# Turning the last four row tiles of x and dO by transposing DMA through DRAM instead of by TensorE, in a gated spectral and GEGLU backward kernel

## The chip, the cores and the metric

One core of a Trainium2 chip runs one launch. The metric is device time in microseconds, the median of several runs; the kernel before took 1384.09 us (three runs, 1383.98 to 1384.36). The profile is one execution of 1384.02 us, whose recorded span is 1382.2 us. The core's engines work at the same time and wait for each other by semaphores: PE (TensorE, matrix products; "PEld" is its weight load), DVE (VectorE), ACT (ScalarE), POOL (GpSimd), and SP (SyncE), which here does nothing but issue DMA transfers. "Granted clock" is the share of full speed that TensorE was given; it was 1.00 throughout.

## The reference

The kernel returns the output of a gated sum of two branches and the gradients of it with respect to x and all weights:

```python
x = A_x                                                   # [2048, 576], bf16
g = sigmoid((x * gate_w).sum(-1, keepdims=True))
a = irfft2(rfft2(x) * (w_r + 1j * w_i))                   # spectral branch
b = (gelu(x @ w_gate) * (x @ w_up)) @ w_down              # GEGLU branch, 4608 inner columns
out = g * a + (1 - g) * b
# returned: out, and the vjp for grad_out (called dO below) with respect to
# x, w_r, w_i, w_gate, w_up, w_down and gate_w
```

For the GEGLU branch each inner column needs the row of x and of dO multiplied with weights. TensorE contracts over the partition, so it needs x and dO with their 576 columns on the partitions: xT and dOT, the "turned" forms. The 2048 rows are cut into 16 row tiles of 128 rows (row p*16+t is row p of tile t), the 576 columns into four interleaved chunks of 128 (column 4*m+r is row m of chunk r) and a tail of 64.

## The kernel before

The inner columns are worked through in 18 groups of 256 (`NG`); each group takes the 16 row tiles in four slots of four tiles (`NPR = 4`, loop variable `m`). A slot multiplies (`H_mm`), evacuates on ACT (`H_da`, `H_act`), and works out the GELU derivative on DVE in two halves (`H_ew1`, `H_ew2`), with a sigmoid on ACT between them. The weight gradients of a group (`W_units`) are filled in between the products of the next group. Group 0 has no such filler: there x and dO are still being turned, four row tiles per slot.

```python
    def H_ew1(g, tiles, da):
        xb, q, hu = tiles
        s = ewt("s", g)
        V.tensor_scalar(s[:], q[:], A_GELU, 1.0, op0=ALU.mult, op1=ALU.add)
        V.tensor_tensor(s[:], xb[:], s[:], op=ALU.mult)
        V.tensor_scalar(q[:], q[:], 6.0 * A_GELU * C_GELU, 2.0 * C_GELU, op0=ALU.mult, op1=ALU.add)
        dH = keep.tile([P, 4, 2, FG], BF16, tag="dH", name="dH")
        V.tensor_tensor(dH[:, :, 0, :], da[:], hu[:], op=ALU.mult)
        return s, dH
    ...
    def H_ew2(g, m, tiles, s, dH, da):
        xb, q, hu = tiles
        one = g < 2 or m == 2
        if one:
            om = xb if g < 2 else ewt("sg", g)
            nc.scalar.activation(s[:], s[:], ACT.Sigmoid, scale=2.0 * C_GELU)
        ...
        def products():
            V.tensor_tensor(dHu, da[:], xb[:], op=ALU.mult)
            V.tensor_tensor(A[:], xb[:], hu[:], op=ALU.mult)
        V.tensor_tensor(xb[:], xb[:], s[:], op=ALU.mult)
        if g < 2:
            products()
        V.tensor_tensor(q[:], xb[:], q[:], op=ALU.mult)
        if one:
            V.tensor_scalar(om[:], s[:], -1.0, 1.0, op0=ALU.mult, op1=ALU.add)
        V.tensor_tensor(om[:], om[:], q[:], op=ALU.mult)
        if g >= 2:
            products()
        V.tensor_tensor(om[:], om[:], s[:], op=ALU.add)
        V.tensor_tensor(dHg, dHg, om[:], op=ALU.mult)
        # then, as a later step: A, dHu and dHg are stored to DRAM
```

Turning by TensorE: three items per four tiles, chunks 0 and 1, chunks 2 and 3, and the tail. Each item needs one of two PSUM buffers "pf" and a copy out of it, on DVE or ACT.

```python
    def titems(src, dst, t0, ps, copies, n=4):
        def item(k, cs):
            def f():
                tp_ = ps[k](BF16).rearrange("p (j t m) -> p j t m", j=2, t=4)
                for j, c in enumerate(cs):
                    for tt in range(n):
                        if c < 4:
                            nc.tensor.transpose(tp_[:, j, tt, :], src[:, t0 + tt, eo(c)], ident[:])
                        ...                          # the tail: one transpose per tile
                copies[k](dst[:, cs[0]:cs[0] + len(cs), t0:t0 + n, :], tp_[:, 0:len(cs), 0:n, :])
            return f
        return [item(k, cs) for k, cs in enumerate(((0, 1), (2, 3), (4,)))]
```

`gate(k)` makes the gate's logits of tiles 4k to 4k+3 out of xT, into another "pf" buffer. A slot of group 0 (engines take instructions in the order in which they are recorded here):

```python
                do2 = items(dB, dOT, m + 2, AC, AC, VC)               # dO, two slots ahead
                x1 = items(xn, xT, m + 1, AC if m else VC, VC, VC)    # x, one slot ahead
                z, xy_full = H_mm(g, m, [lambda: gate(0)] if m == 0 else rest, ...)
                da = H_da(g, m, z)
                ...
                elif m < NPR - 1:
                    early, mid_, late_ = x1[:1], x1[1:], []
                for f in early:
                    f()
                xy = xy_full(0)
                for f in mid_:
                    f()
                if held and m < NPR - 1:
                    held.pop()()                     # H_ew2 of the slot before
                for part in (1, 0):
                    H_act(0, xy, tiles, part)
                if held:
                    held.pop()()
                xy = xy_full(1, between)
                for part in range(2):
                    H_act(1, xy, tiles, part)
                ...
                if m < NPR - 1:
                    gate(m + 1)
                ...
                if m + 2 < NPR:
                    do2[0]()
                    rest = do2[1:]
                state += [*H_ew1(g, tiles, da), da]
                held.append(sigs)
            ...
            if m < 3 and g + 1 < NG:                 # weights of the next group
                for part in ((0, 1), (2,), (3,))[m]:
                    load_w(g + 1, part)
```

`load_w` already turns w_down in the way that the change takes for x and dO: part 1 is a transposing DMA into an SBUF tile, part 2 writes that tile to a DRAM scratch, part 3 reads it back so that four interleaved chunks come out (a row of the scratch is a column of the weight; "(p r) f -> p r f", r=4). All of these are issued from SP. The tile framework hands out eight DMA semaphores in turn, so a DMA of SP is not issued before the one eight before it has landed.

The masked tables ("tails", a helper `D4[2]`): two memsets and 16 small multiplications on POOL, used from the seventh slot on; recorded in the first slot.

Of the kernel before, what the change touches and what calls it, by code (L numbers as in the profile page):

```python
# [11 lines left out]
BF16 = mybir.dt.bfloat16  # L12
# [22 lines left out]
FCH = FG // P  # L35
NUNIT = 18
IMM = bass.MemoryType

# [237 lines left out]
def kernel(  # L276
# [22 lines left out]
    o5v = out_5[0:512, :].rearrange("(c p) f -> p c f", p=P)  # L299
    scr = [[dram.tile([4, P, FF], BF16, name=f"scr{k}_{m}") for m in range(T // 4)] for k in range(3)]  # L300
    wscr = [dram.tile([512, FG], BF16, name=f"wscr{k}") for k in range(2)]
    a_scr = dram.tile([S, D], BF16, name="a_scr")
# [44 lines left out]
    def load_do(t0, n=4):  # L347
        LD.dma_start(dB[:, t0:t0 + n, :], do_v[:, t0:t0 + n, :])

    ident = res.tile([P, P], BF16, name="ident")  # L350
    make_identity(nc, ident[:])
# [8 lines left out]
    for k in range(1, 4):  # L360
        load_do(4 * k)
        load_x(4 * k)
    tb = iotas(nc, res, unit)

# [137 lines left out]
    def H_ew2(g, m, tiles, s, dH, da):  # L502
        xb, q, hu = tiles
        one = g < 2 or m == 2
        if one:
            om = xb if g < 2 else ewt("sg", g)
            nc.scalar.activation(s[:], s[:], ACT.Sigmoid, scale=2.0 * C_GELU)
        else:
            om, s = s, ewt("sg", g)
            nc.scalar.activation(s[:], om[:], ACT.Sigmoid, scale=2.0 * C_GELU)  # L510
            nc.scalar.activation(om[:], om[:], ACT.Sigmoid, scale=-2.0 * C_GELU)
# [6 lines left out]
        V.tensor_tensor(xb[:], xb[:], s[:], op=ALU.mult)  # L518
        if g < 2:
            products()  # L520
# [3 lines left out]
        V.tensor_tensor(om[:], om[:], q[:], op=ALU.mult)  # L524
        if g >= 2:
            products()
# [164 lines left out]
    def turned(h):  # L691

        def f():
# [9 lines left out]
            if h == 1:  # L703
                V.tensor_copy(tb.BT[:].rearrange("p v m -> p (v m)"), tp_[:, 1, 0:2 * P])
            tb.RT.extend(o[:, k, :] for k in range(8))
        return f

# [262 lines left out]
    def opening():  # L970
        x0 = titems(xn, xT, 0, (pgtile, pgtile, phtile), (VC, VC, VC))
        for f in (x0[2], x0[0], x0[1]):
            f()
        parity()
        D4[2]()

# [69 lines left out]
    for g in range(NG):  # L1046
# [3 lines left out]
        for m in range(NPR):  # L1050
# [15 lines left out]
            if g == 0:  # L1066
# [8 lines left out]
                if m == 0:  # L1075
                    early, mid_, late_ = do1[:2], [do1[2], x1[0]], x1[1:]
                elif m < NPR - 1:
                    early, mid_, late_ = x1[:1], x1[1:], []
                else:
                    early, mid_, late_ = [], [], []  # L1080
# [20 lines left out]
                if m == 0:  # L1101
                    build_R(nc, tb, unit, 4)
                    columns_B(nc, tb, res)
                elif m == 1:
                    next(makeB)
                if m < NPR - 1:
                    gate(m + 1)
# [3 lines left out]
                if m + 2 < NPR:  # L1111
                    do2[0]()
                    rest = do2[1:]
                state += [*H_ew1(g, tiles, da), da]
                held.append(sigs)
            else:
# [31 lines left out]
                at, k, free = 0.0, k0, 0.0  # L1148
                last = getattr(upcoming(n - k0)[-1], "last", 0.0) if n > k0 else 0.0
                tables = {6: 2}.get(pr)  # L1150
                for i, (w, f) in enumerate(jobs):
                    if k < n and (at >= max(min(total * k / n - 0.45, total - last - 0.9 * (n - 1 - k)), free) or len(jobs) - i <= n - k):
                        free = at + (1.7 if wide() else 0.0)
# [19 lines left out]
            if m < 3 and g + 1 < NG:  # L1173
                for part in ((0, 1), (2,), (3,))[m]:
                    load_w(g + 1, part)
            if done[0] == n_slots or (pr >= wgT_from and pr % 2 == 0 and len(wgT_all) < 20):
                load_wgT()
# [245 lines left out]
```

## Time and profile before

| what | value |
|---|---|
| time, median of three runs | 1384.09 us (1383.98 to 1384.36) |
| profiled span | 1382.2 us |
| busy: PE, PEld, DVE, ACT, POOL | 99%, 66%, 57%, 51%, 19% of the span |
| 0 to 60 us: PE, DVE, ACT, POOL busy | 56.47, 49.28, 47.57, 26.31 us |
| 60 to 120 us: PE, DVE, ACT, POOL busy | 57.25, 49.86, 48.29, 7.29 us |
| 950 to 1382.2 us: PE, DVE, ACT busy | 428.62, 89.39, 13.92 us |

Lines are named by their number in the kernel (L399 is a transposing matmul of chunks 0 to 3, L405 one of the tail; L406 their copy out of PSUM; L423 the gate; L444 and L449 the product z with dOT; L453 and L460 the product xy with xT; L472, L479, L481, L482 the evacuations on ACT; L487 to L528 the chain on DVE; L507 the sigmoid). Matmuls are pipelined and their ends are modelled: a matmul of 512 columns shows 379 ns but 16 of them in a row start within 3.45 us. Gaps are therefore read from the starts.

In a line of the timeline stand the start in us, the duration in us, engine, line, operation, what is written and read, the shape, and how many instructions were merged; in brackets the idle time before it and what ended it. In the chain of waits (the chain of work that ended last, in order of time) stand start, duration, engine, what is written, line, and the number of instructions.

### The profile page before, as it was taken

To read this page: it belongs to the slowest core of one execution; us is meant where nothing else is said; L and a number is where in the kernel's file an instruction comes from. 1 tells how busy PE (TensorE), PEld (TensorE's weight loads), DVE (VectorE), ACT (ScalarE), POOL (GpSimd) and SP (SyncE) were. 2 spreads that over 40 slices of the span, in tenths; PEclk is the share of its full clock that TensorE was granted. 3 is DMA by queue.
4 is the path that set the end of the run, shared out by engine and by line. 5 is a ranking of instruction groups with operands and counts; after the bars stand their busy time and mean duration, and the time that the engine had idled before them with its cause. 6 is when DMAs were issued, how large, how long until landed. Compare 5 with 4: busy or idle time off the path is not lost.

```text
span 1382.2 us, 25988 instructions
## 1 busy us (share of the span) xinstructions
PE 1363.2 (99%) x10186; PEld 908.5 (66%) x10272; DVE 783.2 (57%) x1514; ACT 701.6 (51%) x1300; POOL 259.8 (19%) x513
## 2 busy tenths in 40 slices
PE   9999999999999999999999999999999999999998
PEld 6556656566556556556656566556777777777776
DVE  7887777865988877885676766550001642122101
ACT  7877777768877877866766767651000000000000
POOL 7001110132445444331110111110000110000000
PEclk9999999999999999999999999999999999999999
DMA  7434444466466665555556556659999997787773
GB/s 234 126 88 136 128 131 119 120 169 158 129 162 159 161 160 150 143 156 151 135 157 154 159 158 166 168 128 274 196 190 197 235 193 164 158 161 168 155 150 88
DMA packets 512423, 218.95 MB, mean 158 GB/s; under 512 B 312010, under 2 KB 503180, under 8 KB 512300
## 3 DMA queue, kind: packets, MB, share of 16 engines
q1 hardware_dynamic: 495178, 191.89, 59.3%
q0 software_dynamic: 14912, 24.24, 6.1%
q8 instruction: 80, 1.31, 0.4%
q10 hardware_dynamic: 2210, 1.15, 0.4%
q14 instruction: 43, 0.35, 0.1%
HBM read 45.51 MB, written 98.30 MB: 104 GB/s over the span
## 4 chain that ended last, share of the span: by engine, by line
PE 92%; ACT 3%; DVE 2%; DMA 1%; issue 1%; ACTq 0%; SPq 0%; DVEq 0%
PE acc L1273 31%; PE wps L590 16%; PE xy L460 16%; PE wps L572 10%; PE z L444 8%; PE wps L604 2%; PE xy L453 2%; PE z L449 2%; DMA wgu<-in_B_w_up_dram 1%; DMA xn<-in_A_x_dram 1%; PE pf L914 1%; PE pf L840 1%; PE pf L751 1%; PE pf L633 1%; PE pf L916 1%
## 5 line engine op out<-in xcount | busy, mean ns | idle before, releaser
L1273 PEld LDWEIGHTS <-pin 128*128 128x128 bf16 x3456 | 337.5, 98 | 86.3 <-issue 0.3
L590 PE MATMUL wps<-dH,xn 128*128 128x512 bf16 x1135 | 270.0, 379 | 0.9
L460 PE MATMUL xy<-wgu,xT 128*128 128x512 bf16 x1083 | 258.6, 380 | 8.2 <-issue 6.8
L460 PEld LDWEIGHTS <-xT 128*128 128x128 bf16 x1152 | 106.4, 98 | 132.9 <-issue 24.8
L590 PEld LDWEIGHTS <-xn 128*128 128x128 bf16 x1152 | 111.4, 98 | 118.4 <-issue 0.6
L1290 ACT COPY bo<-acc 128x288 f32<-128x288 f32 x32 | 12.8, 399 | 305.0 <-PE acc L1273 271.6
L572 PE MATMUL wps<-dB,A 128*128 128x288 bf16 x1152 | 153.3, 286 | 0.1
L597 POOL DMA_DIRECT2D out_dram<-dw x134 | 72.8, 547 | 421.9 <-ACT dw L541 380.4
L1273 PE MATMUL acc<-wgT,pin 128*128 128x288 bf16 x1152 | 143.8, 286 | 0.0
L1273 PE MATMUL acc<-wuT,pin 128*128 128x288 bf16 x1152 | 143.6, 286 | 0.0
L1273 PE MATMUL acc<-wd_all,pin 128*128 128x288 bf16 x1152 | 142.6, 286 | 0.0
L444 PE MATMUL z<-wdT,dOT 128*128 128x256 bf16 x1152 | 137.7, 273 | 0.0
L572 PEld LDWEIGHTS <-A 128*128 128x128 bf16 x1152 | 112.0, 98 | 33.0 <-issue 0.3
L472 ACT ACTIVATE da<-z,omg 128x256 bf16<-128x256 f32 x288 | 112.0, 471 | 31.9 <-PE z L449 31.8
L444 PEld LDWEIGHTS <-dOT 128*128 128x128 bf16 x1152 | 112.3, 98 | 21.6 <-issue 0.6
L1345 DVE SCALAR_TENSOR_TENSOR f32t<-gwf,dlog,b16t 128x576 f32<-128x576 f32 x16 | 13.1, 818 | 171.8 <-DMA b16t<-dxa_scr 171.8
L481 ACT CAST xb<-xy 128x512 bf16<-128x512 f32 x144 | 85.0, 590 | 48.2 <-PE xy L460 48.2
L479 ACT ACTIVATE q<-xy 128x512 bf16<-128x512 f32 x144 | 87.8, 613 | 17.0 <-PE xy L460 13.5
L482 ACT CAST hu<-xy 128x512 bf16<-128x512 f32 x144 | 87.4, 607 | 0.0
L518 DVE TENSOR_TENSOR xb<-xb,sg 128x1024 bf16<-128x1024 bf16 x48 | 33.1, 690 | 85.8 <-ACT sg L510 85.7
L541 ACT CAST dw<-wps 128x512 bf16<-128x512 f32 x72 | 42.3, 590 | 54.8 <-PE wps L590 52.4
L1304 DVE SCALAR_TENSOR_TENSOR b16t<-b16t,g,f32t 128x576 bf16<-128x576 bf16 x16 | 13.1, 818 | 98.1 <-DMA b16t<-a_scr 97.9
(239 smaller groups left out, 1700.3 us busy)
## 6 DMA issues: line engine op xcount, KB each, us to landing
scr<-dH SPq DMA_DIRECT2D x144, 256.0 KB, 3.4
scr<-A SPq DMA_DIRECT2D x72, 256.0 KB, 2.5
out_dram<-dw POOLq DMA_DIRECT2D x134, 64.0 KB, 2.5
wd_all<-in_B_w_down_dram SPq DMA_DIRECT2D x3, 1728.0 KB
out_dram<-dwd POOLq DMA_DIRECT2D x34, 144.0 KB, 2.9
scr_p<-Vt SPq DMA_DIRECT2D x32, 145.0 KB, 2.8
wgu<-in_B_w_gate_dram SPq DMA_DIRECT2D x18, 256.0 KB, 4.1
wgu<-in_B_w_up_dram SPq DMA_DIRECT2D x18, 256.0 KB, 3.4
```

Source lines behind the costliest of these rows:

```text
L444: nc.tensor.matmul(zo(t), lhsT=dOT[:, ci, t, :], rhs=wdT[:, ci, :], start=(t % 4 < 2 and ci == 0), stop=False)
L460: nc.tensor.matmul(xy[k][:, t % 2, :], lhsT=xT[:, ci, t, :], rhs=wgu[:, ci, :], start=False, stop=(ci == 3))
L472: nc.scalar.activation(da[:, t, :], z[:, t % 2, t // 2, :], ACT.Copy, scale=omg32[:, 4 * m + t:4 * m + t + 1])
L479: nc.scalar.activation(q[:, h, :], xy[:, :, 0:FG], ACT.Square)
L481: nc.scalar.copy(xb[:, h, :], xy[:, :, 0:FG])
L482: nc.scalar.copy(hu[:, h, :], xy[:, :, FG:2 * FG])
L518: V.tensor_tensor(xb[:], xb[:], s[:], op=ALU.mult)
L541: wcopy[0](out, in_)
L572: nc.tensor.matmul(wps[:, :288], lhsT=tl(0, t)[:, fch * P:(fch + 1) * P], rhs=dB[:, t, h * 288:(h + 1) * 288], start=(t == 0), stop=(t == ...
L590: nc.tensor.matmul(wps[:].rearrange("p a b -> p (a b)"), lhsT=xn[:, t, c * P:(c + 1) * P], rhs=kt[t // 4][1][:, t % 4].rearrange("p k f -> ...
L597: wst[0].dma_start(ov[:, c, fsl], dw[:, k, :])
L1273: nc.tensor.matmul(acc[:, :288], lhsT=src[:, r, :], rhs=w_of(r)[:, h * 288:(h + 1) * 288], start=(first and r == 0), stop=(last and r == F ...
```

## The change

Of the last four row tiles (12 to 15) the chunks 0 to 3 of x and of dO are no longer turned by TensorE. Eight transposing DMAs, one per tile and tensor, are issued right behind the loads; each brings 128 rows by 512 columns, turned, into one of four SBUF tiles. In slot 0 the four tiles are written to DRAM, in slot 1 they are read back into xT and dOT, four interleaved chunks at a time. The tails of these tiles are still turned by TensorE. This is for TensorE, ACT and DVE to have less to do in group 0. Besides, the masked tables are recorded in slot 1 and no longer in slot 0; the second group's chain on DVE takes the order that the third and later groups have (products later, into a tile of its own); and the rule that spreads the transform's units over a slot's weight gradient work is given one more hint.

```diff
+LT = T - 4
...
+    turn = [[dram.tile([512, 2 * P], BF16, name=f"turn{k}_{u}") for u in range(2)] for k in range(2)]
...
+    byq = {}
+    def load_turned(part):
+        for k, (v, dst) in enumerate(((do_v, dOT), (x_v, xT))):
+            for u in range(2):
+                if part == 0:
+                    tmp = byq[k, u] = unit([4, 2, P], name="turn")
+                    for j in range(2):
+                        LD.dma_start_transpose(tmp[:, :, j, :], v[:, LT + 2 * u + j, 0:512])
+                elif part == 1:
+                    LD.dma_start(turn[k][u][:].rearrange("(c p) f -> p c f", p=P),
+                                 byq[k, u][:].rearrange("p c t m -> p c (t m)"))
+                else:
+                    LD.dma_start(dst[:, 0:4, LT + 2 * u:LT + 2 * u + 2, :].rearrange("p r t m -> p r (t m)"),
+                                 turn[k][u][:].rearrange("(p r) f -> p r f", r=4))
...
     for k in range(1, 4):
         load_do(4 * k)
         load_x(4 * k)
+    load_turned(0)
     tb = iotas(nc, res, unit)
...
-            om = xb if g < 2 else ewt("sg", g)
+            om = xb if g == 0 else ewt("sg", g)
...
-        if g < 2:
+        if g == 0:
             products()
...
-        if g >= 2:
+        if g > 0:
             products()
...
+        f.room, f.last = 1.7, 2.0                    # the unit that turns the transform's tables
...
         parity()
-        D4[2]()
...
                 elif m < NPR - 1:
-                    early, mid_, late_ = x1[:1], x1[1:], []
+                    early, mid_, late_ = (x1[:1], x1[1:], []) if m < NPR - 2 else ([], x1[2:], [])
...
                 elif m == 1:
                     next(makeB)
+                    D4[2]()
...
                 if m + 2 < NPR:
-                    do2[0]()
-                    rest = do2[1:]
+                    rest = do2[1:] if m + 3 < NPR else do2[2:]
+                    if len(rest) > 1:
+                        do2[0]()
...
-                last = getattr(upcoming(n - k0)[-1], "last", 0.0) if n > k0 else 0.0
+                ups = upcoming(n - k0)
+                last = getattr(ups[-1], "last", 0.0) if ups and (n < 5 or hasattr(ups[-1], "wide")) else 0.0
+                due = [total - last - sum(getattr(u, "room", 0.9) for u in ups[j:-1]) for j in range(len(ups))]
...
-                    if k < n and (at >= max(min(total * k / n - 0.45, total - last - 0.9 * (n - 1 - k)), free) or len(jobs) - i <= n - k):
+                    if k < n and (at >= max(min(total * k / n - 0.45, due[k - k0]), free) or len(jobs) - i <= n - k):
...
                 for part in ((0, 1), (2,), (3,))[m]:
                     load_w(g + 1, part)
+                if g == 0 and m < 2:
+                    load_turned(m + 1)
```

## The prediction

> **What bounds the kernel now.** I read the page's busy times first, then the chain of waits, the timelines and the list of waits of the first 120 us, because everything that the change touches lies there: the instruction streams of the two programs, laid side by side without line numbers, differ only in slots 0 to 7 and in the place of four weight gradient products near the unit that turns the transform's tables.
>
> ```profile
> PE 1363.2 (99%) x10186; PEld 908.5 (66%) x10272; DVE 783.2 (57%) x1514; ACT 701.6 (51%) x1300; POOL 259.8 (19%) x513
> ```
>
> TensorE sets the end: nothing later can give back or take what it loses early. But in the first 95 us it is not alone. The chain of waits of 28 to 46 us:
>
> ```profile
> 28.45 0.61 DVE q L521
> 29.07 0.02 issue
> 29.09 1.13 DVE xb L523
> ...
> 34.45 0.35 DVE dOT L406
> 34.80 0.04 issue
> 34.84 0.61 PE pf L399 x8
> ...
> 37.40 0.48 PE pf L423 x20
> 37.88 1.77 PE z L444 x16
> ...
> 40.56 1.69 PE xy L460 x7
> ...
> 43.84 0.95 ACT s L507
> ...
> 44.82 0.70 DVE xb L518
> ```
>
> The reader is to see a ring. From 25.5 us DVE works without a break; its copy of a turned tail at 34.45 frees the PSUM buffer that the last transposes of x wait for (34.84); behind them come the gate (37.40), z and xy of slot 3, then ACT, whose sigmoid releases DVE at 44.82, where DVE had sat idle for 1.07 us (timeline). From there DVE's chain gives dH of slot 2 at 50.08, and the timeline has the first weight gradient product of group 0 start at 50.08. So what slot 3 gains, the rest gains, up to DVE's own pace.
>
> The timeline of SP shows how the same kind of turning goes for the weights:
>
> ```profile
> 18.75 1.22 SPq L335 DMA_TRANSPOSE wdT<-in_B_w_down_dram  x1
> 20.55 1.43 SPq L336 DMA_TRANSPOSE wtmp<-in_B_w_down_dram  x1
> 23.35 0.50 SPq L339 DMA_DIRECT2D wdT<-wdT  x1
> 25.55 0.40 SPq L340 DMA_DIRECT2D wscr<-wtmp  x1
> 27.87 0.33 SPq L342 DMA_DIRECT2D wdT<-wscr  x1
> ```
>
> One such turn takes from 20.55 to about 30: 5.0 us to the write, 2.3 us to the read, some 2.3 us to land. At 20.5 us the loads of x and dO have only just landed (the transpose at 20.55 waited for the last load of xn).
>
> And the stage in which the second group's chain matters:
>
> ```profile
> 88.96 0.60 ACT L479 ACTIVATE q<-xy 128x512 bf16<-128x512 f32 x1 [1.52 <-DVE xb L524]
> ```
> ```profile
> 90.14 0.41 PE L651 MATMUL pf<-Y,Rt 128*128 128x292 bf16 x2 [1.07 <-ACT Y L640]
> 90.39 1.02 PE L590 MATMUL wps<-dH,xn 128*128 128x512 bf16 x4
> 92.16 0.42 PE L633 MATMUL pf<-Dt,xT 128*128 128x146 bf16 x4 [0.75 <-ACT ve L655]
> ```
>
> ACT's square of the next slot overwrites q, which DVE's L524 still has to read; it comes 1.52 us late, and TensorE then stands for ACT twice, 1.07 and 0.75 us.
>
> **What the Trainium skill says.** The page "DMA: Bandwidth & Descriptors", section "Rules for kernel authors", says that a DMA that reads what an earlier DMA wrote must be issued only after the earlier one's completion semaphore. The trace agrees: SP waited 1.6 us for the transpose before it wrote the scratch at 25.55. The page's section "Anatomy of one DMA" gives about 2.0 us of fixed cost per transfer, most of it the write's receipt (for the GpSimd path); in this trace a 256 KB store from SP landed 2.3 us after its issue. So each of the three hops costs over 2 us however few its bytes. The page "Perfetto Trace Analysis", section "Identifying the Most-Contended Engine", warns that matmul occupancy is a poor measure because matmuls are pipelined. The trace agrees: 56.47 us of the first 60 read busy, though the starts show holes. The page "GPSIMD Engine Reference", section "Specifications", says that GpSimd and VectorE share SBUF interfaces. Here L523 took 1.12 us beside an IOTA of POOL at 29.05, against 0.43 us otherwise; but beside the 16 small products of the masked tables (13.93 to 23.85) DVE's operations kept their usual 0.42 to 0.43 us.
>
> **The change, part by part.**
>
> Removed from TensorE: 32 transposes (4 tiles, 4 chunks, 2 tensors), in four bursts of 8 at 27.76, 29.96, 31.67 and 34.84. A burst shows 0.61 us, but pushes what follows by 0.45 us (27.76 to 28.21): 4 x 0.45 = 1.8 us. To this comes the wait of 0.83 us before the burst at 34.84. ACT loses three copies (2.15 us for two, 1.04 us for one: 3.2 us), DVE one, about 0.6 us of the 1.02 us for two at 35.48.
>
> Where would slot 3 begin without any DMA? z of slot 2 at 27.75; plus z 1.75, tail transposes 0.22, z tail 0.33, xy tail 0.43, xy 1.73, tail 0.22, xy 1.73 = 34.2 us for the gate (before 37.40 in the chain). DVE: its chain from 26.44 is unchanged to 34.45, then two tail copies of 0.35 us, so the next half starts at 35.2 instead of 36.42, and DVE would be ready for slot 2's second half at 35.2 + 5.2 + 2.1 = 42.5 against 44.82: 2.3 us is the most that DVE lets through.
>
> Added, on SP and the DMA engines: eight transposes behind the loads. With eight semaphores the k-th waits for the load eight before it; the loads' landings can be read off the SP waits of before, where weight loads stood in those places (11.8, 14.5, 15.8, 17.3, 18.7, 20.5 us). The eighth is therefore issued at about 20.5 and ends its issue at 21.8 (1.22 to 1.43 us each). They are 1.05 MB; in the last stage, where transposes fill the queue, the DMA engines moved 181 GB/s at about 0.87 busy, so about 205 GB/s: 5.1 us, to about 25.7. The weight loads of group 1, six issues, wait for these one by one and go out at 22 to 26, the two weight transposes at 26 to 28.4. Then the four writes to DRAM, 0.45 us each, 28.4 to 30.2. Next in SP's order stands the write of the weights' scratch, which waits for wtmp: 27.0 + 4.6 = 31.6 us. Behind it the four reads, 0.45 us apart: issued 32.1, 32.5, 33.0, 33.4; landed after about 2.3 to 2.8 us, dOT at 34.6 and 35.1, xT at 35.6 and 36.2.
>
> The gate of slot 3 needs xT of the last tiles (its weight loads wait for exactly these two reads). It is held from 34.8 (after DVE's tail copy) to about 36.2, z follows at 36.7 against 37.88 in the chain: **1.2 us gained in slot 3**, not the 2.3 us that DVE would let through.
>
> The second group: the new order has L524 fourth in the half instead of sixth, with the two products (0.61 us each) behind it. q is free 1.2 to 1.4 us earlier. At 75.46 ACT had waited 0.60 us and at 88.96 1.52 us for it. TensorE's waits behind it were 1.07, 0.75, and 0.23 us at 103.71: 2.05 us, of which I expect about 1.3 to go, as ACT has its own work up to there. DVE also saves some dependent neighbours (starts 0.72 us apart when dependent, 0.61 otherwise): about 0.2 us in a slot, mostly hidden.
>
> The masked tables later on POOL: nothing waits for them before 75 us, and they would end at about 40. The IOTA that hurt L523 moves to an earlier time; up to 0.7 us either way on DVE, counted as nothing. The hint for the turning unit moves four products in front of or behind one wait of 0.2 us: 0.1 us.
>
> **Sum:** 1.2 + 1.3 + 0.1 = 2.6 us off 1384.09, taken down to 2.4 us for disturbances: **1381.7 us**. After 120 us TensorE's stream is the same and its starts are dense, so the gain is carried to the end.
>
> **The rivals.** (1) The wait moves from DVE to DMA altogether: the hops come some 2 us later than worked out, xT at 38 or later, and slot 3 starts no earlier than before. For it: SP is one queue in order, and each landing above holds the next issue; the loads keep the DMA engines over 0.99 busy to 20 us. Against it: after 20 us they are 0.4 busy, so there is room. It would leave 1.4 us of gain, 1382.7; with xT at 39.5, a loss of 2 us in slot 3 and about 1384.8. (2) The buffers: the four SBUF tiles are taken from the pool of 18 units and come around again in slots 1 to 3, so DVE's first operation of slot 1's chain (32.3 us before) now waits for the first write to DRAM (issued about 28.4, landed about 31). If that landed at 34, DVE would be late by 2 us; the 1.2 us that slot 3 is DMA-bound would absorb half. About 1383. (3) The DMA is hidden altogether (transposes run beside the loads, or land in 3 us as the fastest of wtmp did): slot 3 gains the full 2.3 us, then ACT and DVE bound it; with the second group 1380.3. (4) ACT bounds at 75 to 92 us on its own (two table loads of 1.28 us and the sines stand there), so that the new order buys only 0.5 us: 1382.5.
>
> **Range and chances.** The four outcomes lie between 1380 and 1385. I take 1379.9 to 1384.0 for 8 in 10; most weight is on a gain of 1 to 4 us. 2% are 27.7 us; the change touches work of some 3 us, so within 2% is all but certain.
>
> **What would show it.** Right: no transposes at the four places, the gate of slot 3 waiting for a DMA with its start at 35 to 37 us; DVE's idle time of 1.07 us before slot 2's second half still there in part; the first weight gradient product near 49; the waits of TensorE at 90 and 92 us together under 1 us. Wrong: the gate starts after 37.4 (rival 1); DVE waits for a DMA at 32 us (rival 2); the gate waits for DVE instead (rival 3); ACT's square at 88 us without a wait and TensorE still waiting (rival 4). A time above 1384 would mean that the turned tiles came later than TensorE would have made them.

## The result and the profile after

The changed kernel takes **1391.53 us** (median of six runs, 1390.39 to 1392.77) against 1384.42 us for the kernel before on the same chip (six runs): ratio 1.005, interval 1.0037 to 1.0063. It is 7.1 us slower; 2.4 us faster (1381.7 us) was predicted. The profiled execution took 1392.77 us, the longest of the six and 1.2 us over the median, so the profile shows a loss of 8.8 us (spans 1391.0 and 1382.2).

The page of the kernel after: busy times, and the granted clock in 40 slices.

```profile
PE 1373.4 (99%) x10240; PEld 909.0 (65%) x10240; DVE 781.0 (56%) x1513; ACT 699.4 (50%) x1297; POOL 259.6 (19%) x513
...
PEclk9899999999999999999999999999999999999999
```

DVE and ACT are busy 2.2 us less each (the prediction had 0.6 us for DVE and 3.2 us for ACT). TensorE has 32 transposes less to do and reads 10.2 us *more* busy, but that difference is not a measure of anything: in the profile before, 86 of the 10272 matmuls have no record (PE shows x10186, PEld x10272), 69 of them of 512 columns in the product xy, and their time stands there as idle; after, none is missing (x10240 both). What does speak is the second slice of the clock, which has an 8: for a while the matmuls were slower.

SP's timeline of the kernel after (its own instructions; start, duration, line, what is moved, how many):

```profile
11.21 8.84 SPq L361 DMA_TRANSPOSE turn<-in_grad_out_dram  x4
20.09 6.22 SPq L361 DMA_TRANSPOSE turn<-in_A_x_dram  x4
26.36 0.60 SPq L332 DMA_DIRECT2D wgu<-in_B_w_gate_dram  x1
...
31.55 2.33 SPq L338 DMA_TRANSPOSE wtmp<-in_B_w_down_dram  x1
33.92 2.84 SPq L363 DMA_DIRECT2D turn<-turn  x4
36.88 0.82 SPq L341 DMA_DIRECT2D wdT<-wdT  x1
37.80 0.74 SPq L342 DMA_DIRECT2D wscr<-wtmp  x1
38.60 1.28 SPq L366 DMA_DIRECT2D dOT<-turn  x2
39.92 1.30 SPq L366 DMA_DIRECT2D xT<-turn  x2
41.27 0.62 SPq L344 DMA_DIRECT2D wdT<-wscr  x1
```

The reader is to add start and duration: each line ends where the next begins. From 11.2 to 41.9 us SP issues without a pause, and the two reads of xT are nearly the last in the row. In the chain of waits of the kernel after, SP's pieces stand ahead of the landing of xT (start, duration, engine, what, line, count; the first three are the longest issues of a transpose of dO and x):

```profile
12.78 3.58 SPq L361
...
17.79 2.26 SPq L361
...
21.41 2.28 SPq L361
...
40.60 4.98 DMA xT<-turn
...
46.05 3.44 PE z L464 x16
```

TensorE's timeline of the kernel before has the gate of slot 3 (L423), z of slot 3 and z of the second group at

```profile
37.23 0.64 PE L423 MATMUL pf<-gwT,xT 128*128 128x1 bf16 x20
37.74 1.91 PE L444 MATMUL z<-wdT,dOT 128*128 128x256 bf16 x16
...
43.80 1.91 PE L444 MATMUL z<-wdT,dOT 128*128 128x256 bf16 x16
```

That of the kernel after shows the wait in brackets and the slow slot (gate L443, z of slot 3 at 45.91, z of the second group at 54.64):

```profile
43.88 0.43 PE L443 MATMUL pf<-gwT,xT 128*128 128x1 bf16 x10 [8.80 <-DMA xT<-turn]
45.62 0.43 PE L443 MATMUL pf<-gwT,xT 128*128 128x1 bf16 x10 [1.32 <-DMA xT<-turn]
45.91 3.57 PE L464 MATMUL z<-wdT,dOT 128*128 128x256 bf16 x16
...
54.64 1.91 PE L464 MATMUL z<-wdT,dOT 128*128 128x256 bf16 x16
```

The same 16 matmuls take 3.57 us at 45.91 and 1.91 us at 54.64. From z of slot 3 to z of the second group it is 54.64 - 45.91 = 8.73 us; before, 43.80 - 37.74 = 6.06 us. The windows of the kernel after say why (stretch; sum of its us, busy us of PE, PEld, DVE, ACT, POOL, each with its count; then the granted clock, the DMA engines' share, GB/s):

```profile
36.00:38.00 2.00, 0.00 (x0) 0.00 (x0) 1.08 (x3) 0.00 (x0) 1.76 (x4) 0.98 1.05 294
38.00:42.00 4.00, 0.00 (x0) 0.00 (x0) 3.97 (x9) 3.93 (x7) 1.29 (x2) 0.50 0.90 252
42.00:46.00 4.00, 0.81 (x21) 0.73 (x22) 3.76 (x8) 0.04 (x1) 0.00 (x0) 0.50 1.08 311
46.00:50.00 4.00, 4.00 (x24) 2.57 (x23) 0.93 (x2) 0.57 (x3) 0.00 (x0) 0.50 0.98 293
```

After some 3 us of waiting TensorE's clock falls to 0.50 (near 37.9 us) and stays there for the first 5.7 us of the work that the late tiles let go (to 51.6 us, by the means of narrower windows).

At 84 to 104 us the new order of the second group's chain did its work: of the waits of 1.07, 0.75 and 0.23 us before, one above 0.5 us is left in the timeline of TensorE of the kernel after:

```profile
101.67 0.42 PE L653 MATMUL pf<-Dt,xT 128*128 128x146 bf16 x4 [0.64 <-ACT ve L675]
```

Followed along the same landmarks, TensorE is late by 6.65 us at the gate of slot 3 (43.88 against 37.23), 8.17 at z, 10.84 at z of the second group, still 10.84 at 81 us, and 9.51 at the next slot's z (94.77 before, 104.28 after). Past that some 0.7 us more comes back by the end.

### The profile page after: what moved, and what is told of

It is laid out like the page before. It is cut to its first block, busy times and chain, and to the rows that moved or that the text cites. A ratio compares the mean times of both kernels' runs of the same rounds, so it can differ in the third digit from the quotient of the medians.

```text
span 1391.0 us, 26030 instructions
## 1 busy us (share of the span) xinstructions
PE 1373.4 (99%) x10240; PEld 909.0 (65%) x10240; DVE 781.0 (56%) x1513; ACT 699.4 (50%) x1297; POOL 259.6 (19%) x513
## 3 DMA queue, kind: packets, MB, share of 16 engines
q10 hardware_dynamic: 2210, 1.15, 0.3%
## 4 chain that ended last, share of the span: by engine, by line
PE 93%; SPq 2%; ACT 2%; DVE 1%; DMA 1%; issue 0%; ACTq 0%; DVEq 0%
PE acc L1299 30%; PE wps L610 17%; PE xy L480 17%; PE wps L592 10%; PE z L464 8%; PE wps L624 2%; PE xy L473 2%; PE z L469 2%; SPq L361 1%; PE pf L653 1%; PE pf L935 1%; PE pf L861 1%; PE pf L772 1%; PE pf L937 1%; PE pf L671 1%; PE pf L656 1%
## 5 line engine op out<-in xcount | busy, mean ns | idle before, releaser
L480 PE MATMUL xy<-wgu,xT 128*128 128x512 bf16 x1152 | 270.9, 380 | 0.0
```

The lines of the kernel that those rows point to most:

```text
L480: nc.tensor.matmul(xy[k][:, t % 2, :], lhsT=xT[:, ci, t, :], rhs=wgu[:, ci, :], start=False, stop=(ci == 3))
```

## The experiments

A table first, so that the single runs can be read beside each other. All times are us. The four landmarks are starts on TensorE in each run's profiled execution (of the gate, the start of its last part where a wait splits it); the time is the median. The ratio, with its interval, is to executions of the kernel before on the same chip, whose medians lay between 1384.09 and 1384.42. free_tiles ran once and has no ratio.

| run | gate of slot 3, last part | z of slot 3 | z of the second group | first weight gradient | time | ratio |
|---|---|---|---|---|---|---|
| before | 37.23 | 37.74 | 43.80 | 50.08 | 1384.42 | |
| after | 45.62 | 45.91 | 54.64 | 60.92 | 1391.53 | 1.005 (1.0037 to 1.0063) |
| rest_only | 36.62 | 37.13 | 43.19 | 49.47 | 1381.26 | 0.9977 (0.9968 to 0.9986) |
| free_tiles | 34.37 | 35.06 | 41.12 | 47.75 | 1379.74 | |
| chain_only | 37.26 | 37.76 | 43.82 | 50.11 | 1382.73 | 0.9988 (0.9981 to 0.9995) |
| kept_busy | 51.66 | 52.17 | 58.23 | 64.51 | 1395.40 | 1.0077 (1.006 to 1.0094) |
| kept_warm | 45.25 | 45.51 | 51.57 | 57.85 | 1389.71 | 1.0036 (1.0023 to 1.0048) |
| copies_on_pool | 41.47 | 41.75 | 50.34 | 56.62 | 1387.47 | 1.002 (1.0013 to 1.0028) |
| turned_unused | 44.50 | 45.08 | 51.45 | 57.73 | 1387.70 | 1.0023 (1.0015 to 1.0032) |
| own_buffers | 45.12 | 45.41 | 53.65 | 59.93 | 1391.62 | 1.0045 (1.003 to 1.006) |
| turn_first | 44.69 | 45.20 | 51.26 | 57.54 | 1388.33 | 1.0029 (1.0018 to 1.0039) |
| turn_first_own | 36.49 | 36.75 | 46.73 | 54.43 | 1385.59 | 1.0005 (0.9996 to 1.0013) |
| dO_only | 36.34 | 36.85 | 42.91 | 49.19 | 1381.12 | 0.9974 (0.9965 to 0.9984) |
| x_only | 36.26 | 36.52 | 42.58 | 48.86 | 1381.04 | 0.9975 (0.9964 to 0.9985) |

**What is each part worth?** *rest_only*: the change without the turning by DMA (`load_turned` is never called, the last four tiles are turned by TensorE).

```diff
-    load_turned(0)
...
-                    early, mid_, late_ = (x1[:1], x1[1:], []) if m < NPR - 2 else ([], x1[2:], [])
+                    early, mid_, late_ = x1[:1], x1[1:], []
...
-                    rest = do2[1:] if m + 3 < NPR else do2[2:]
-                    if len(rest) > 1:
-                        do2[0]()
+                    do2[0]()
+                    rest = do2[1:]
...
-                if g == 0 and m < 2:
-                    load_turned(m + 1)
```

> All of the change but the turning by DMA: TensorE turns all 16 row tiles as before; only the later masked tables, the second group's chain and the hint for the table-turning unit are in. Theory (the loss is the late turned tiles alone, the rest of the change helps as predicted): 1.2 to 1.5 us below before, that is 1382.7 to 1383.2, with TensorE's waits for ACT near 90 us (1.07 and 0.75 us before) down to under 0.8 us together. Rival (the reordered chain or the tables on POOL cost too, and part of the 7 us is theirs): at or above 1384.4.

It measured 1381.26 us, below the range expected. So the turning by DMA alone costs 1391.53 - 1381.26 = 10.3 us, and the rest gains 2.8 us, twice what I had given it. Part of that is a DVE operation that I had counted as nothing. DVE's timeline of the kernel before, and then of rest_only:

```profile
29.09 1.12 DVE L523 TENSOR_SCALAR xb<-s 128x1024 bf16<-128x1024 bf16 x1
```
```profile
29.11 0.43 DVE L542 TENSOR_SCALAR xb<-s 128x1024 bf16<-128x1024 bf16 x1
```

With the masked tables recorded later, POOL's IOTA no longer lies beside this operation: 0.69 us of DVE in the stretch where TensorE waits for DVE, and z of slot 3 starts 0.61 us earlier. In chain_only below, where the tables stay in slot 0, L523 takes 1.12 us and z stays at 37.76.

*chain_only*: the kernel before with only the second group's new order.

```diff
-            om = xb if g < 2 else ewt("sg", g)
+            om = xb if g == 0 else ewt("sg", g)
...
-        if g < 2:
+        if g == 0:
             products()
...
-        if g >= 2:
+        if g > 0:
             products()
```

> The kernel before with only the second group's chain in its new order. Theory A, my step of 1.3 us: TensorE's waits at 90 and 92 us fall from 1.82 us to under 1 us, and the time is 1382.8. Theory B, ACT bounds that stretch with its own work: 0.5 us, 1383.6. Theory C, the chain makes the whole gain of the version without turning DMA, 2.8 us: 1381.3.

1382.73 us, 1.4 us less than the 1384.10 of the kernel before in this comparison: theory A. Of the waits named, TensorE's timeline of chain_only has left

```profile
90.87 0.42 PE L633 MATMUL pf<-Dt,xT 128*128 128x146 bf16 x4 [0.64 <-ACT ve L655]
```

The wait for Y (1.07 us) is gone, and the one for ve fell from 0.75 to 0.64. The 1.5 us between chain_only and rest_only are the 0.6 us of the masked tables, a wait of 0.2 us at the unit with the hint that is gone in rest_only, and some 0.6 us that come in small steps after 290 us and that I could not tie to a line.

*free_tiles*: the changed kernel without any transposing DMA, and nothing in its place. It leaves out the turning of the chunks 0 to 3 of the last four tiles: these are set to zero once at the start.

```diff
-    load_turned(0)
...
+    for dst in (xT, dOT):
+        nc.gpsimd.memset(dst[:, 0:4, LT:T, :], 0.0)
...
-                if g == 0 and m < 2:
-                    load_turned(m + 1)
```

> The changed kernel with the turning DMAs taken out and the four tiles' chunks 0 to 3 of xT and dOT left at zero: TensorE, ACT and DVE do the work of the changed kernel, no transfer is waited for, and the output is wrong in those rows by intent. It shows what the removed work is worth. Theory (DVE lets 2.3 us of slot 3 through, the second group 1.3 us): 1380.5 to 1381.2, the gate of slot 3 near 34.8 us. Rival (TensorE's removed work is worth nothing there, DVE or ACT bounds group 0 anyway): no better than the kernel with the rest of the change alone, 1383.

1379.74 us in a single run; TensorE's timeline of free_tiles:

```profile
34.37 0.83 PE L442 MATMUL pf<-gwT,xT 128*128 128x1 bf16 x20
35.06 1.91 PE L463 MATMUL z<-wdT,dOT 128*128 128x256 bf16 x16
```

This is the ceiling: with tiles turned for nothing, slot 3 starts 2.07 us earlier than in rest_only and the kernel ends 1.5 us earlier. The whole scheme plays for 1.5 us, and pays 10 us for tiles that come late.

**Is the clock a cost of its own?** *kept_busy*: the changed kernel with idle matmuls ahead of the last gate.

```diff
     def gate(k):
         lps = pgtile()
         ts = slice(4 * k, 4 * k + 4)
+        for _ in range(46 if k == 3 else 0):
+            nc.tensor.matmul(lps[:], lhsT=ident[:], rhs=wts[0][0][:, 0, :], start=True, stop=True)
```

> The changed kernel with 46 idle products of 512 columns (about 10 us) put before the gate of slot 3 on TensorE, into the gate's own PSUM buffer and overwritten: TensorE is busy while it waits for the turned tiles, nothing else changes. Theory (after the wait of 10 us TensorE runs at a granted clock of 0.5 to 0.9, and z and xy of slot 3 take 8.7 us instead of 6.1): 2.3 to 2.7 us better than the changed kernel, about 1389, with the clock at 1.00 from 40 to 60 us. Rival (the clock costs nothing since DVE and ACT bound that stretch, or it does not drop for idleness): within 0.7 us of the changed kernel, 1391.

It missed its aim. The filler wrote into the gate's own PSUM buffer, which DVE had not emptied, because DVE itself was waiting. TensorE's timeline of kept_busy:

```profile
38.81 13.01 PE L442 MATMUL pf<-wgu,ident 128*128 128x512 bf16 x46 [4.22 <-DVE dOT L426]
...
52.17 1.91 PE L466 MATMUL z<-wdT,dOT 128*128 128x256 bf16 x16
...
58.23 1.91 PE L466 MATMUL z<-wdT,dOT 128*128 128x256 bf16 x16
```

It began late, ran partly at half speed and outlasted the landing of xT. But behind it the slot took 58.23 - 52.17 = 6.06 us again. *kept_warm* is the same with the filler in the next z's buffer, free early:

```diff
+        if k == 3:
+            wz = pz.tile([P, 2, 2, FG], F32, tag="z", name="z")
+            for i in range(46):
+                nc.tensor.matmul(wz[:, i % 2].rearrange("p a f -> p (a f)"), lhsT=ident[:], rhs=wts[0][0][:, 0, :], start=True, stop=True)
         lps = pgtile()
```

> The changed kernel with 46 idle products of 512 columns (0.21 us each, 9.8 us in all) ahead of the last gate, this time into the PSUM buffer of the next z, which ACT has read long before, so that they start near 35 us and end near 45, before the last x tile lands at 45.6. If the fall of TensorE's clock to 0.50 is what makes slot 3 take 8.73 us instead of 6.06, slot 3 takes 6.1 us here and the time falls by 2.7 us to 1388.8. Rival: slot 3 is slow because TensorE reads SBUF beside the saturated DMA engines; then it still takes 8.7 us and the time stays at 1391.5.

TensorE's timeline of kept_warm:

```profile
34.29 10.09 PE L442 MATMUL z<-wgu,ident 128*128 128x512 bf16 x45
...
45.25 0.40 PE L447 MATMUL pf<-gwT,xT 128*128 128x1 bf16 x10 [0.41 <-DMA xT<-turn]
45.51 1.91 PE L468 MATMUL z<-wdT,dOT 128*128 128x256 bf16 x16
...
51.57 1.91 PE L468 MATMUL z<-wdT,dOT 128*128 128x256 bf16 x16
```

xT lands nearly as late as in the changed kernel (0.4 us earlier), and the slot takes 51.57 - 45.51 = 6.06 us with the DMA engines as full as there (shares 1.12 from 44 to 46 us and 1.15 from 46 to 48; 1.09 and 1.15 in the changed kernel) and the clock at 1.00. So the rival, TensorE slowed by full DMA engines, is out, and the slow slot was the clock: 8.73 - 6.06 = 2.67 us. The medians differ by 1.8 us (1391.53 to 1389.71), less than expected; the profiled spans differ by 3.1 us (1391.0 to 1387.9), since the profiled execution of the changed kernel is 1.2 us over its median. Work for nothing makes the kernel faster here, which is a diagnosis and no cure.

**Why do the tiles come so late?** *copies_on_pool*: the four writes and four reads are issued from POOL's queue in slot 0.

```diff
-                    LD.dma_start(turn[k][u][:].rearrange("(c p) f -> p c f", p=P),
+                    ST.dma_start(turn[k][u][:].rearrange("(c p) f -> p c f", p=P),
...
-                    LD.dma_start(dst[:, 0:4, LT + 2 * u:LT + 2 * u + 2, :].rearrange("p r t m -> p r (t m)"),
+                    ST.dma_start(dst[:, 0:4, LT + 2 * u:LT + 2 * u + 2, :].rearrange("p r t m -> p r (t m)"),
...
                     build_R(nc, tb, unit, 4)
+                    load_turned(1)
+                    load_turned(2)
...
-                if g == 0 and m < 2:
-                    load_turned(m + 1)
```

> The changed kernel with the four writes to DRAM and the four reads back issued from GpSimd's queue in slot 0, and no longer from SP behind the next group's weights; the transposes stay on SP. Theory (what came late is SP's queue: 8 transposes, 6 weight loads, 2 weight transposes and 4 writes stand before the reads, one after the other): the reads go out at 29 to 32 us, xT lands at 33 to 36, the gate starts by 36, TensorE keeps its clock, and the time falls by 9 to 11 us to 1380.5 to 1382.5. Rival (the DMA engines themselves are the limit, 0.98 to 1.09 busy from 34 to 48 us): the same transfers still need that time, xT lands at 41 or later, and the time stays above 1386.

1387.47 us: 4 us of the 10 come back, and it is the rival that came true, with the last part of the gate at 41.47 us and a time above 1386. POOL issued the xT reads at 30.7 and 32.1 us, 9.2 and 8.5 us before SP did in the changed kernel. But they landed late. The DMA issues of copies_on_pool at 26 to 44 us (what, count, KB each, median us to landing):

```profile
dOT<-turn POOLq DMA_DIRECT2D x2, 256.0 KB, 6.4
xT<-turn POOLq DMA_DIRECT2D x2, 256.0 KB, 8.2
```

A second queue does not give a second set of DMA engines, which is what the Trainium skill says in "DMA: Bandwidth & Descriptors", section "Issuing engines are not separate DMA queues". The run fits it: the engines were full from 30 to 34 us (shares 1.05 and 1.45; 288 GB/s from 32 to 34), and the transpose of the weights that SP issued at 29.99 us took 7.1 us to land as well. What delayed the reads, the weights ahead of them at the engines or POOL's own kind of queue (the profile lists it as software_dynamic, SP's as hardware_dynamic), this run does not separate.

*turn_first*: SP issues the writes and reads ahead of the second group's weights.

```diff
+                if g == 0 and m == 0:
+                    load_turned(1)
+                    load_turned(2)
                 for part in ((0, 1), (2,), (3,))[m]:
                     load_w(g + 1, part)
-                if g == 0 and m < 2:
-                    load_turned(m + 1)
```

> The changed kernel, but SyncE issues the four writes to DRAM and the four reads back ahead of the second group's weights, not between and behind them. Theory A, the place in SyncE's queue makes the turned tiles late: the writes go out at about 26.5 to 29.5, the reads at 31 to 34, xT lands at 37 to 38 and the gate starts there, 6 to 7 us earlier; the second group's weights are then late instead (its last wdT read near 46, landed near 48), so that TensorE waits some 3 us ahead of z of the second group: 1386 to 1388. Theory B, the DMA engines are the bound: xT lands at 42 or later although its reads are issued by 34, and the time stays within 1 us of 1391.5 or gets longer.

1388.33 us, and neither theory: xT no longer held anything, nor did the second group's weights, and yet slot 3 began at 45.2 us. The waits of 26 to 62 us of turn_first (engine, line, waited for: us in total, times, longest):

```profile
DVE XR L191 <- DMA turn<-turn: 10.3, 1, 10.3
...
PE pf L419 <- DVE dOT L426: 8.5, 1, 8.5
```

DVE stands 10.3 us for a write to DRAM. That is the second rival of the prediction: the transposed tiles lie in buffers of a pool that goes round, and the next user of the buffer is DVE. In the changed kernel another operation of DVE has such a wait of 4.4 us, and the longer wait for xT hides it:

```profile
36.82 0.43 DVE L507 TENSOR_SCALAR s<-q 128x1024 bf16<-128x1024 bf16 x1 [4.44 <-DMA turn<-turn]
```

*turned_unused* measures the side effects without the wait for the data: TensorE turns everything as before (the two edits of rest_only that put this back are in it, not shown below), and the transposing DMAs and the writes to DRAM run too, but nothing reads their result (the four reads back are left out).

```diff
                 for part in ((0, 1), (2,), (3,))[m]:
                     load_w(g + 1, part)
-                if g == 0 and m < 2:
-                    load_turned(m + 1)
+                if g == 0 and m == 0:
+                    load_turned(1)
```

> TensorE turns all tiles as before; the eight transposing DMAs and the four writes to DRAM run as in the change, but the reads back are left out, so nobody uses their result. It shows what the DMA traffic costs when its data are not waited for. Theory A, the side effects are not small: DVE's first operation of slot 1's chain still waits for the first write to DRAM until about 36.8 (4.4 us), slot 3 starts near 40, and the time is 1384.5 to 1386 against 1381.3 without the DMAs. Theory B, only the late data count: 1381.3 to 1382.

1387.70 us: 6.4 us over rest_only, more than theory A had it. DVE's timeline and then TensorE's, of turned_unused (its profiled execution is the longest of its twelve, 1389.45 us):

```profile
37.21 0.53 DVE L507 TENSOR_SCALAR s<-q 128x1024 bf16<-128x1024 bf16 x1 [5.29 <-DMA turn<-turn]
```
```profile
39.85 1.01 PE L419 MATMUL pf<-ident,xn 128*128 128x128 bf16 x8 [5.66 <-DVE dOT L426]
...
41.09 3.62 PE L480 MATMUL xy<-wgu,xT 128*128 128x512 bf16 x8
```

The wait is handed on from DVE to TensorE, whose clock falls in it: the eight matmuls at 41.09 take 3.62 us, where rest_only needs 1.89 us for eight. Wait and clock together are what the run shows; it does not price the buffers apart from the traffic of the twelve transfers.

*own_buffers*: the changed kernel, with the transposed tiles in two dH buffers that are not needed before slot 6 (the write to DRAM and the place of `load_turned(0)` follow suit, not shown).

```diff
-                    tmp = byq[k, u] = unit([4, 2, P], name="turn")
+                    if u == 0:
+                        byq[k] = keep.tile([P, 4, 2, FG], BF16, tag="dH", name="turn")
+                    tmp = byq[k, u] = byq[k][:, :, u, :].rearrange("p c (t m) -> p c t m", t=2)
```

> The changed kernel, but the four transposed tiles lie in two buffers of the dH pool that nothing needs before slot 6, not in units of the pool that DVE's chain uses. DVE's wait of 4.4 us for the first write to DRAM goes. Theory A, the two late things lie side by side and the later one counts: the gate still waits for xT until 45.6, and the time stays at 1391 to 1392. Theory B, DVE's lateness adds to the end on its own: the first weight gradient product, at 60.92 us in the changed kernel, comes 1.5 us earlier or more, and the time is 1389 to 1390.

1391.62 us, no change: DVE's wait is gone from the list, and the gate still waits for xT until 45.12 us. Theory A.

*turn_first_own*: both repairs at once, that is the edits of own_buffers and of turn_first.

> Both repairs at once: writes and reads ahead of the second group's weights, and transposed tiles in buffers of their own. Theory A, these are the two waits and each hides the other: TensorE goes on at 25 us without the wait of 8.5 us for DVE, xT lands at 36 to 37.2 and the gate of slot 3 starts there, at full clock; then the second group's weights are late (last wdT read issued at 44, landed near 47), so that z of the second group starts at 46 to 47 against 43.19 in the version without turning DMA: 1384 to 1386. Theory B, a third wait on the DMA engines takes over: the gate starts after 40, and the time is 1388 or more.

1385.59 us: theory A, but for the full clock. TensorE's timeline of turn_first_own:

```profile
35.65 0.40 PE L445 MATMUL pf<-gwT,xT 128*128 128x1 bf16 x10 [1.13 <-DMA xT<-turn]
36.49 0.40 PE L445 MATMUL pf<-gwT,xT 128*128 128x1 bf16 x10 [0.43 <-DMA xT<-turn]
36.75 3.24 PE L466 MATMUL z<-wdT,dOT 128*128 128x256 bf16 x16
...
46.73 3.02 PE L466 MATMUL z<-wdT,dOT 128*128 128x256 bf16 x16 [2.14 <-DMA wdT<-wscr]
```

Slot 3 begins where the prediction had put it (36.7 us). Two pairs of runs each differ in one thing only. The order of SP's queue: xT is there at 45.1 us in own_buffers and at 36.5 us here. The buffers: 1388.33 us in turn_first, 1385.59 us here. And the reads of x, issued at 30.2 and 31.3 us from SP and ahead of the weights, took 5.4 us to land, against 8.2 us from POOL at nearly the same time and behind the weights. Now the second group's weights pay: their last read goes out at 43.67 us and TensorE waits 2.14 us for it. And the clock falls twice, although no wait was long. The windows of turn_first_own (columns as above):

```profile
36.00:37.00 1.00, 0.57 (x16) 0.49 (x14) 1.00 (x2) 1.00 (x3) 0.93 (x2) 1.00 0.61 166
37.00:38.00 1.00, 1.00 (x8) 0.73 (x6) 0.93 (x3) 0.50 (x3) 0.93 (x2) 0.57 0.72 193
38.00:39.00 1.00, 1.00 (x7) 0.67 (x6) 0.97 (x2) 0.00 (x0) 0.91 (x2) 0.50 0.35 69
```

**Is half the turning in time?** *dO_only* and *x_only* turn one tensor by DMA and the other by TensorE (for the other, the edit of rest_only that gives its items back is in, not shown).

```diff
-        for k, (v, dst) in enumerate(((do_v, dOT), (x_v, xT))):
+        for k, (v, dst) in enumerate(((do_v, dOT),)):            # dO_only
+        for k, (v, dst) in enumerate(((x_v, xT),)):              # x_only
```

> Only dO's last four tiles are turned by DMA (four transposes, two writes, two reads); x's are turned by TensorE as before; the rest of the change is in. Theory A, a queue of half the length is in time: the transposes' issue ends near 20, the reads go out near 31 and land by 35, z of slot 3 does not wait, and the time is 1380.5 to 1381 (0.3 to 0.8 under the version without any turning DMA, 1381.26). Theory B, even half of the traffic comes behind the loads and the weights: z of slot 3 waits for dOT until 38 to 41, and the time is 1383 to 1386.

> Only x's last four tiles are turned by DMA, dO's by TensorE; the rest of the change is in. x's turning takes a copy from DVE, dO's takes only copies from ACT, and DVE is what slot 3 waits for. As in the version that turned only dO, the reads should go out near 29.4 and 30 and land by 35. Theory A: the gate starts at 35 to 35.5, 1 us earlier than in the version without turning DMA, and the time is 1380.0 to 1380.9, the best of all. Theory B: the gate needs xT some 2 us earlier than z needs dOT, so that it waits to 36.5 or later, and the time is 1381.3 or more.

1381.12 and 1381.04 us: both beat the kernel before, and neither is clear of rest_only (1381.26; the three intervals overlap almost wholly). dO_only lies just outside theory A's 1380.5 to 1381. With half the queue the four transposes end their issue at 19.3 to 19.4 us and the reads go out at 29.35 and 30.0, so in slot 3 no DMA holds TensorE up by more than 0.41 us. x_only starts the weight gradient products 0.61 us earlier than rest_only. But four of its eight executions took 1380.2 to 1380.5 and four 1381.6 to 1382.2; the profiled one is of the upper four, and its waits of the last stage show

```profile
PE acc L1298 <- DMA pin<-scr: 1.1, 1, 1.1
```

a wait that rest_only's profile does not have. Whether x_only is the better kernel stays open; theory A's range (1380.0 to 1380.9) holds for half of its runs.

## Why the prediction was wrong, point by point

**The step that failed is the timetable of SP and the DMA engines**: "the eighth is therefore issued at about 20.5 and ends its issue at 21.8", and what followed from it, down to "xT at 35.6 and 36.2". Term by term:

| term | predicted | measured in the kernel after |
|---|---|---|
| eight transposes: end of issue | 21.8 | 26.3 (1.26 to 3.58 us each) |
| weight loads and weight transposes: from there to the end | 6.6 us (to 28.4) | 7.6 us (to 33.9) |
| four writes | 1.8 us (to 30.2) | 2.84 us (to 36.8) |
| scratch of the weights, until the first read goes out | 1.9 us (to 32.1) | 1.8 us (to 38.6) |
| last xT read issued | 33.4 | 40.6 |
| last xT read landed after | 2.8 us | 4.98 us |

4.5 us come from the first line. I had the eighth transpose wait for the last load (20.5 us) and then take 1.3 us, the issue time of two transposes in a calmer stage. SP waited for no load: it was issuing from 11.2 us on, and the eight issues took 15.1 us, 1.9 us each on the mean. Five took 1.26 to 1.5 us, near what I had; three took 2.26 to 3.58 us, and what stretched those is not shown. The remaining 2.7 us of issue are single lines of 0.6 to 0.7 us where I had put 0.45 us, and weight transposes of up to 2.33 us. The landing is slower by 2.2 us, beside DMA engines that were partly idle before and are full by then (0.90 to 1.08 in the windows); that this is the reason is likely, and no run shows it by itself. Of the two grounds the order of SP's queue is the larger: with the same transfers in the other order (turn_first_own against own_buffers) xT is there 8.6 us earlier, though the landing still takes 5.4 us.

**A term was missing**: TensorE's clock. I had no line for it, since the profile before has none below full speed. The Trainium skill has it in "TensorE: Matmul & The Clock Gate", section "Part 1: The HAM clock gate (the "warmup" mystery)": half rate after about 3.4 us of idleness, full rate after about 3.4 us of work. The size of the step agrees: in the seven profiles in which the clock fell it was at 0.50, the only lower value, for 3.4, 6.8, 10.2 or 13.7 us (from the means of their windows). The delay is not a fixed one: the fall came 2.2 to 5.0 us after TensorE had run out of full products, 2.8 us in the changed kernel, and in turn_first_own a gap of 2.1 us was enough, less than the page asks for; here the measurement decides. Its worth is 2.67 us in slot 3 (kept_warm). A wait for a late tile of over 2 us should be priced with that on top.

**The sum, as it came out** (profiled spans): 10.84 us lost at z of the second group, against 1.2 gained in the prediction; of it 8.17 are late tiles and 2.67 the clock. Then 1.33 us back at 94 us, and 0.7 us later: 8.8 us.

**What was right.** The ceiling: "34.2 us for the gate" without any DMA (34.37 in free_tiles). The second group's order: 1.3 us, measured 1.33 in the changed kernel and 1.4 by itself. "nothing later can give back" holds for what slot 3 lost: behind it came only the 1.33 us and the 0.7 us in small steps. That nothing later can take is less sure: x_only's profile loses 1.1 us to a DMA in the last stage, and why it does is not known.

**What was mis-sized.** The masked tables: "counted as nothing", worth 0.6 us. The row from which it follows (L523 at 1.12 us) was in the prediction, and so was the chain in which it stands. The hint, "0.1 us": 0.2 us are seen, and some 0.6 us more are not located.

**The rivals.** Rival 1 ("the wait moves from DVE to DMA altogether") is what happened. I gave it too little room, xT at 39.5 as the worst. My ground against it, "after 20 us they are 0.4 busy, so there is room", was read off a kernel without the added transfers, and it left out the queue that feeds the engines. Both count: in the changed kernel the reads are not issued before 38.6 us, and in copies_on_pool, where they are issued 8.5 to 9.2 us earlier, the engines are full and xT still lands at 41.5. Rival 2 (the borrowed buffers) also came about, with DVE waiting 4.4 us at 36.8 us. It cost nothing, for the reason given there (rival 1 absorbs it), but I had sized it at 1 to 2 us, and where nothing hides it the kernel loses 6.4 us to it, the slow clock and the traffic together (turned_unused). Rival 3 did not happen. Rival 4 holds in small part: a wait of 0.64 us for ve stays whatever the order, but the order bought 1.33 us and not 0.5.

## What to carry to other kernels

Lay out the issuing queue like an engine: add up the issue times of everything ahead of the transfer that somebody waits for, in order, with durations from the same crowded stage, before asking whether the DMA engines have room; then ask that too, with the added transfers counted in. Where two waits run side by side, take both away in one experiment as well as singly: own_buffers alone gave nothing, turn_first alone 3.2 us and a new wait, both together 5.9. And price a wait of TensorE of more than 2 us with the slow clock that can follow it.

## What the hardware showed that I had not expected

- A transposing DMA of 128 rows by 512 columns took SP 1.26 us to issue at best and 3.58 us at worst in the changed kernel; eight took 15.1 us, 1.9 us on the mean, against 0.6 us for a plain load of weights right behind them.
- TensorE's clock also fell after a short gap: in turn_first_own it was at 0.50 from about 37.1 us, although only 2.2 us lay between its last product of 512 columns (to 34.5 us) and z (36.75 us), with small gate products in between; and again from about 47.4 us, after a gap of 2.1 us ahead of z at 46.73. Each time it stayed there for 3.4 us. In the kernel before, gaps of 0.83 us at 34 us and of 1.07 us at 89 us left it at 1.00.
- Reads issued from POOL at 28.8 to 32.1 us, behind the weights at the DMA engines, took 6.4 (dO) and 8.2 us (x) to land in copies_on_pool; the same reads issued from SP at 28.8 to 31.3 us, ahead of the weights, took 4.4 and 5.4 us in turn_first_own.
